# First batch of a spectral filter and a two-layer network: products kept whole, work shared out anew between Pool and DVE, one constant on another DMA queue

## The chip, the cores and the metric

One core of one Trainium2 chip. The time is the device time of one execution in microseconds (us), of which I give the median of a kernel's timed runs. The experiments ran in three groups of rounds, each on its own chip (e1 to e4, e5 to e8, e9 to e11), with the kernel before in every round, so times are compared within a group, and between groups only as ratios to the kernel before. Engines are named as in the profile: PE (matmul), DVE (VectorE), ACT (ScalarE), Pool (GpSimd), SP (which only issues DMAs here).

## The reference

A real FFT along the sequence, a product with a complex filter, the inverse FFT, then two dense layers with a leaky ReLU between them:

```python
# x: (8, 3008, 256), filt_r, filt_i: (1505, 256), w_in: (256, 2048), w_out: (2048, 256), all float32
X = np.fft.rfft(x, axis=1)
Y = X * (filt_r + 1j * filt_i)[None]
h = np.fft.irfft(Y, n=3008, axis=1).reshape(24064, 256) @ w_in
out = np.maximum(0.01 * h, h) @ w_out
```

## The kernel before

The transform of length 3008 is split as 94 x 32: matmuls with constant matrices (S1, S2, back with SA and SB), 32x32 transposes on DVE between them, the filter as an elementwise product between S2 and SA. Batches 1 to 7 go through these stages beside the dense layers of the batch before. Batch 0 has nothing to hide behind: its stages are the prologue, written by hand and in program order on every engine. Its 24 frequency groups come in two halves of the feature dimension (`hf` 0 and 1). For each half, PE makes S2 into PSUM; then the two products with `fa` and `fb` are taken either by DVE, straight from PSUM, or by Pool, after ACT has copied PSUM to SBUF; then PE makes SA from both products and ACT casts the result into `big[2]`; DVE transposes that (four transposes, two per half of the features), PE makes SB, and the dense layers begin.

PSUM has two wide buffers of two banks (`ph`) and three single banks (`pf`), used in turn; a matmul into one waits until the last reader of that buffer is done. Dummy matmuls (`keep_warm`) run while PE would stand still.

```python
    filt_load(fa_sb, filt_r, DH, DH, 64)               # the last of 12 filter pieces, all on Pool's queue
    filt_load(fb_sb, filt_i, DH, DH, 64)
    nc.gpsimd.dma_start(i1_sb[:], i1_d.ap())           # constant for SB, 752 KB
    nc.gpsimd.dma_start(w_in_sb[:], ...)
    # ... S1 of batch 0, with dummies ...
    t1_part(0, 0, True)(), t1_part(0, 1, True)()       # DVE: first transposes, half 0
    upper(0)                                           # fa copied on ACT, fb on DVE
    first_s2(0, 0, 8, False)                           # (half, first group, groups, on Pool?)
    first_s2(0, 8, 8, True)
    x_load(1)
    t1_part(0, 2, True)()
    keep_warm(4)
    first_s2(0, 16, 4, False)
    first_s2(0, 20, 4, True)
    t1_part(0, 3, True)()
    first_sa(0, 0), first_sa(0, 16)
    keep_warm(3)
    first_s2(1, 0, 8, False)
    first_s2(1, 8, 8, True)
    first_sa(0, 8), first_sa(0, 20)
    keep_warm(2)
    nc.gpsimd.dma_start(w_out_sb[:], ...)
    first_s2(1, 16, 8, False)
    first_sa(1, 0)
    keep_warm(4)
    first_t2(0), first_t2(1)                           # DVE: second transposes
    first_sa(1, 16), first_sa(1, 8)
    first_t2(2), first_t2(3)
```

## Time and profile before

| | before |
|---|---|
| median of 6 runs (us) | 782.97 (782.36 to 783.17) |
| span of the profiled run | 781.3 |
| first transpose of batch 0 starts at | 17.24 |
| last filter piece lands at | 28.21 |
| second transposes start at | 34.21 |
| first dense matmul at | 42.02 |

From 42 us on PE is the bound and hardly ever stops, so the table's last line is what a change of the prologue can move. The chain of waits and DVE's timeline are in the prediction.

### The profile page before, as it was taken

What the parts mean: (1) busy time and instruction counts of PE and PEld (TensorE: products, weight loads), DVE (VectorE), ACT (ScalarE), POOL (GpSimd) and SP (SyncE); (2) the same over time, 40 slices, a digit from 0 to 9 for tenths busy, and PEclk for the clock granted to TensorE, in tenths of its full rate; (3) what the DMA queues carried; (4) which work ended last, traced back from release to release, by engine and by line L of the source; (5) the groups of instructions that cost most, each with busy time, mean ns of one, the idle gap of its engine ahead of it and who ended that gap; (6) DMA issues with size and microseconds to landing.
All of it is one profiled execution on the core that took longest, in us unless ns stands there. A gap on an engine that the chain in (4) does not pass through costs nothing.

```text
span 781.3 us, 13416 instructions
## 1 busy us (share of the span) xinstructions
PE 772.2 (99%) x5716; PEld 524.0 (67%) x5716; DVE 367.4 (47%) x462; ACT 551.0 (71%) x784; POOL 152.2 (19%) x126
## 2 busy tenths in 40 slices
PE   9899999999999999999999999999999999999998
PEld 4366676666776677666777667766677666766666
DVE  4879751865238641577307754087432765200000
ACT  4587768676787767777587775967668776666664
POOL 5964300340004300042001410025000340000000
PEclk9999999999999999999999999999999999999999
DMA  9963002301041101510105010140101001100111
GB/s 183 228 107 78 32 28 64 86 30 40 33 102 42 42 28 42 108 42 28 41 28 122 28 40 30 41 107 28 42 29 41 28 28 42 41 35 34 41 41 55
DMA packets 39386, 44.15 MB, mean 57 GB/s; under 512 B 11266, under 2 KB 37506, under 8 KB 38658
## 3 DMA queue, kind: packets, MB, share of 16 engines
q0 software_dynamic: 13136, 17.78, 13.4%
q1 hardware_dynamic: 26192, 25.53, 9.3%
q8 instruction: 44, 0.72, 0.4%
q14 instruction: 14, 0.11, 0.1%
HBM read 35.67 MB, written 24.64 MB: 77 GB/s over the span
## 4 chain that ended last, share of the span: by engine, by line
PE 94%; DMA 2%; POOL 1%; ACT 1%; DVE 1%; issue 1%; POOLq 0%
PE ph L376 41%; PE po_ps L390 41%; PE pf L176 3%; PE pf L243 2%; PE pf L231 2%; PE pf L216 2%; DMA x_sb<-in_x_dram 1%; DMA fa_sb<-in_filt_r_dram 1%; PE pf L390 1%; POOL fy_h_c L276 1%; ACT big L187 0%; DVE big L297 0%; ACT big L290 0%; ACT gt_c L381 0%; PE ph L306 0%
## 5 line engine op out<-in xcount | busy, mean ns | idle before, releaser
L381 ACT ACTIVATE gt_c<-ph 128x1024 f16<-128x1024 f32 x376 | 384.8, 1023 | 195.6 <-PE ph L376 194.4
L376 PE MATMUL ph<-yt,w_in_sb 128*128 128x512 f16 (+3 forms) x1600 | 386.4, 366 | 0.3
L390 PE MATMUL po_ps<-w_out_sb,gt_c 128*128 128x256 f16 x2944 | 381.4, 272 | 0.5 <-ACT ost_c_t L397 0.5
L390 PEld LDWEIGHTS <-gt_c 128*128 128x128 f16 x3008 | 290.8, 98 | 89.2 <-issue 1.8
L376 PEld LDWEIGHTS <-w_in_sb 128*128 128x128 f16 x1600 | 154.5, 98 | 95.7 <-issue 0.4
L224 POOL TENSOR_TENSOR y_b_g<-p_b_g,p_b_g 128x512 f16<-128x512 f32 x84 | 106.8, 1271 | 225.4 <-DVE p_b_g L222 225.4
L199 DVE STREAM_TRANSPOSE big<-big 128x1024 f32<-128x1024 f32 x32 | 55.9, 1848 | 126.1 <-ACT big L187 126.1
L187 ACT CAST big<-pf 128x512 f16<-128x512 f32 x186 | 106.4, 604 | 1.8 <-PE pf L256 1.8
L246 DVE CAST yt<-pf 128x376 f16<-128x376 f32 x112 | 56.4, 545 | 86.0 <-PE pf L243 86.0
L220 DVE TENSOR_TENSOR p_b_g<-pf,fa_sb 128x512 f32<-128x512 f32 x84 | 58.1, 692 | 38.0 <-PE pf L216 35.4
L397 ACT COPY ost_c_t<-po_ps 128x256 f32<-128x256 f32 x184 | 69.3, 377 | 6.6 <-PE po_ps L390 5.4
L207 DVE STREAM_TRANSPOSE big<-big 128x1024 f32<-128x1024 f32 x28 | 51.1, 1939 | 34.1 <-ACT big L187 34.1
L221 DVE TENSOR_TENSOR p_b_g<-pf,fb_sb 64x512 f32<-64x512 f32 x84 | 58.2, 693 | 1.1
L222 DVE TENSOR_TENSOR p_b_g<-pf,fb_sb 64x512 f32<-64x512 f32 x84 | 57.4, 684 | 1.1
L132 POOL DMA_DIRECT2D x_sb<-in_x_dram x12 | 6.6, 553 | 253.1 <-PE pf L176 252.3
L243 PEld LDWEIGHTS <-big 128*128 128x128 f16 x448 | 25.6, 98 | 13.2
L176 PE MATMUL pf<-x_sb,f_sb 94*128 94x256 f16 x224 | 33.9, 272 | 0.2 <-DVE yt L246 0.2
L216 PE MATMUL pf<-big,small_sb 128*128 128x512 f16 x84 | 31.8, 379 | 0.0
L231 PE MATMUL pf<-y_b_g,small_sb 128*128 128x512 f16 x84 | 31.8, 379 | 0.0
L176 PEld LDWEIGHTS <-f_sb 94*128 94x128 f16 x224 | 21.5, 97 | 12.4 <-issue 0.4
L243 PE MATMUL pf<-i_sb,big 128*128 128x94 f16 x448 | 28.7, 206 | 0.0
L318 PE MATMUL po_ps<-idle 128*128 128x512 f16 x72 | 18.8, 405 | 1.2 <-DVE one L165 1.2
(46 smaller groups left out, 158.5 us busy)
## 6 DMA issues: line engine op xcount, KB each, us to landing
out_dram<-ost_c_t SPq DMA_DIRECT2D x92, 256.0 KB, 2.1
x_sb<-in_x_dram POOLq DMA_DIRECT2D x6, 1536.0 KB, 11.2
x_sb<-in_x_dram POOLq DMA_DIRECT2D x3, 480.0 KB, 9.8
fa_sb<-in_filt_r_dram POOLq DMA_DIRECT2D x6, 192.0 KB, 10.7
fb_sb<-in_filt_i_dram POOLq DMA_DIRECT2D x6, 192.0 KB, 8.6
w_in_sb<-in_moe_w_in_dram POOLq DMA_DIRECT2D x1, 1024.0 KB, 12.7
w_out_sb<-in_moe_w_out_dram POOLq DMA_DIRECT2D x1, 1024.0 KB, 12.7
x_sb<-in_x_dram POOLq DMA_DIRECT2D x1, 1024.0 KB, 8.1
```

What stands on the lines that cost most here:

```text
L176: nc.tensor.matmul(ps[:, j, :], f1_sb[:N1, n2, :], x_sb[:N1, n2, :], start=True, stop=True)
L187: copy(paired(dst)[:, ds(n0, nn), ds(e0, de)], ps.rearrange("p n (e t) -> p n e t", t=2))
L220: nc.vector.tensor_tensor(p1[:], ps, fa, AL.mult)
L221: nc.vector.tensor_tensor(p2[0:64], ps[64:P], fb[64:P], AL.mult)
L222: nc.vector.tensor_tensor(p2[64:P], ps[0:64], fb[0:64], AL.mult)
L224: nc.gpsimd.tensor_tensor(y1[:], p1[:], p2[:], AL.add)
L243: nc.tensor.matmul(ps[:, j, :], src[:, dt, n2, :], i1_sb[:, n2, :], start=True, stop=True)
L246: copy(yv[:, :, ds(4 * h, 4)], ps.rearrange("p c a -> p a c"))
L376: nc.tensor.matmul(ph[:, j, ds(o, ln)], w_in_sb[:, dt, ts(ct, P)], yt[:, dt, ds(lo, ln)], start=(dt == 0), stop=(dt == NDT - 1),)
L381: nc.scalar.activation(gts[ci][:, ds(2 * g, 2), :], ph, AF.Lrelu)
L390: nc.tensor.matmul(po, gts[ci][:, ct, ts(tj, P)], w_out_sb[:, ct, :], start=(ct == 0), stop=(ct == NCT - 1))
L397: nc.scalar.copy(ost[:, tj % 2, :], po)
```

## The change

The intent is to take load off Pool, which carried the middle of the prologue: Pool gets one chunk of eight groups per half and PE forms that chunk first; the rest of S2 goes to DVE in single banks; the products of a half stay together in the two buffers that the first dense layer uses later; the constant for SB leaves Pool's queue, and the issue of the weights comes after Pool's first products.

```diff
-    nc.gpsimd.dma_start(i1_sb[:], i1_d.ap())
-    nc.gpsimd.dma_start(w_in_sb[:], ...)
...
+    prods = [gtp.tile([P, 2, NC, DH], FP16, tag="gt", padded_shape=[P, 2, Q, DH], ...) for hf in range(2)]
...   # first_s2 takes the kind of PSUM buffer, writes prods[hf][:, i, ds(c, n), :]
     t1_part(0, 0, True)(), t1_part(0, 1, True)()
+    nc.vector.memset(i1_sb[:, 0, 0:2], 0.0)           # holds the load back until DVE is here
+    nc.sync.dma_start(i1_sb[:], i1_d.ap())
     upper(0)
+    first_s2(0, 8, 8, "ph", True)
+    nc.gpsimd.dma_start(w_in_sb[:], ...)
     t1_part(0, 2, True)()
+    first_s2(0, 0, 8, "ph")
+    for n0 in (0, N2 // 2):
+        x_load(1, n0, N2 // 2)
+    t1_part(0, 3, True)()
+    first_s2(0, 16, 4, "pf"), first_s2(0, 20, 4, "pf")
     keep_warm(4)
+    first_s2(1, 0, 8, "ph")
+    first_sa(0, 0, 8)
+    first_s2(1, 8, 8, "ph", True)
+    nc.gpsimd.dma_start(w_out_sb[:], ...)
+    first_sa(0, 16), first_sa(0, 20), first_sa(0, 8, 8)
+    first_s2(1, 16, 4, "pf"), first_s2(1, 20, 4, "ph")
+    first_sa(1, 0, 8)
     keep_warm(3)
     first_t2(0), first_t2(1)
+    first_sa(1, 16), first_sa(1, 20), first_sa(1, 8, 8)
     first_t2(2), first_t2(3)
...   # the old order removed
```

More of the change, by code (lines that the diff above doesn't have):

```diff
@@ L158 @@
     filt_load(fb_sb, filt_i, DH, DH, 64)
-    nc.gpsimd.dma_start(i1_sb[:], i1_d.ap())
-    nc.gpsimd.dma_start(w_in_sb[:], moe_w_in.rearrange("(dt p) c -> p dt c", p=P))
     idle = cpool.tile([P, CH], FP16, name="idle")
@@ L258, in first_s1, with first_s2 @@
         spread(big[0], n0, ps, copy)
-    def first_s2(hf, c, n, on_pool):
-        ps = bank("ph", n, DH)
+    prods = [gtp.tile([P, 2, NC, DH], FP16, tag="gt", padded_shape=[P, 2, Q, DH], name=f"prod{hf}")
+             for hf in range(2)]
+    def first_s2(hf, c, n, kind, on_pool=False):
+        ps = bank(kind, n, DH)
         src = paired(big[1])
@@ L267, in first_s2 @@
         fs = [f[:, ds(c, n), ts(hf, DH)] for f in (fa_sb, fb_sb)]
+        y = [prods[hf][:, i, ds(c, n), :] for i in range(2)]
         if on_pool:
-            y = [outp.tile([P, n, DH], FP16, tag="ost", name=f"fy{i}_h{hf}_c{c}") for i in range(2)]
             xs = [scrp.tile([P, 4, DH], FP32, tag=f"p{j // 4 + 1}", name=f"fx_h{hf}_c{c + j}")
@@ L277, in first_s2, with first_sa @@
         else:
-            y = [ypp.tile([P, n, DH], FP16, tag=f"yw{i}", bufs=2, name=f"fy{i}_h{hf}_c{c}")
-                 for i in range(2)]
             for i in range(2):
-                nc.vector.tensor_tensor(y[i][:], ps, fs[i], AL.mult)
-        ys[(hf, c)] = y
-    def first_sa(hf, c):
-        y = ys.pop((hf, c))
-        for j in range(0, y[0].shape[1], 4):
+                nc.vector.tensor_tensor(y[i], ps, fs[i], AL.mult)
+    def first_sa(hf, c, n=4):
+        y = [prods[hf][:, i, ds(c, n), :] for i in range(2)]
+        for j in range(0, n, 4):
             ps = bank("pf", 4, DH)
@@ L329 @@
     t1_part(0, 0, True)(), t1_part(0, 1, True)()
+    nc.vector.memset(i1_sb[:, 0, 0:2], 0.0)
+    nc.sync.dma_start(i1_sb[:], i1_d.ap())
     upper(0)
-    first_s2(0, 0, 8, False)
-    first_s2(0, 8, 8, True)
-    x_load(1)
+    first_s2(0, 8, 8, "ph", True)
+    nc.gpsimd.dma_start(w_in_sb[:], moe_w_in.rearrange("(dt p) c -> p dt c", p=P))
     t1_part(0, 2, True)()
-    keep_warm(4)
-    first_s2(0, 16, 4, False)
-    first_s2(0, 20, 4, True)
-    t1_part(0, 3, True)()
-    first_sa(0, 0), first_sa(0, 16)
-    keep_warm(3)
-    first_s2(1, 0, 8, False)
-    first_s2(1, 8, 8, True)
-    first_sa(0, 8), first_sa(0, 20)
-    keep_warm(2)
-    nc.gpsimd.dma_start(w_out_sb[:], moe_w_out.rearrange("(ct p) d -> p ct d", p=P))
-    first_s2(1, 16, 8, False)
-    first_sa(1, 0)
-    keep_warm(4)
+    first_s2(0, 0, 8, "ph")
[3 more added lines that the diff above has]
+    first_s2(0, 16, 4, "pf"), first_s2(0, 20, 4, "pf")
+    keep_warm(4)
+    first_s2(1, 0, 8, "ph")
+    first_sa(0, 0, 8)
+    first_s2(1, 8, 8, "ph", True)
+    nc.gpsimd.dma_start(w_out_sb[:], moe_w_out.rearrange("(ct p) d -> p ct d", p=P))
+    first_sa(0, 16), first_sa(0, 20), first_sa(0, 8, 8)
+    first_s2(1, 16, 4, "pf"), first_s2(1, 20, 4, "ph")
+    first_sa(1, 0, 8)
+    keep_warm(3)
     first_t2(0), first_t2(1)
-    first_sa(1, 16), first_sa(1, 8)
+    first_sa(1, 16), first_sa(1, 20), first_sa(1, 8, 8)
     first_t2(2), first_t2(3)
```

## The prediction

> **What bounds the kernel now.** I read the page first, for where the time is, then the chain of waits for the first 45 us, since every changed line lies there, then the timeline engine by engine from 19 to 42 us. The page:
>
> ```profile
> PE 772.2 (99%) x5716; PEld 524.0 (67%) x5716; DVE 367.4 (47%) x462; ACT 551.0 (71%) x784; POOL 152.2 (19%) x126
> PE 94%; DMA 2%; POOL 1%; ACT 1%; DVE 1%; issue 1%; POOLq 0%
> ```
>
> PE is busy 99% of the span and holds 94% of the chain that ended last; the rest of that chain, some 5%, is the prologue, in which the first batch goes through its transforms before the dense layers have anything to do. The first dense matmul starts at 42.02 us and from there PE rarely stops (before line 376 it waited 0.3 us in all). So whatever moves that start moves the end by as much, and nothing else in this change can. The chain of waits in the prologue (columns: start us, us, what):
>
> ```profile
> 12.00 9.73 DMA fa_sb<-in_filt_r_dram
> 22.02 0.70 POOL w_in_sb L160
> 22.83 3.07 POOL fy_h_c L276 x3
> 26.19 1.17 POOL fy_h_c L276
> 27.36 0.53 POOL x_sb L132
> 27.91 2.29 POOL fy_h_c L276 x2
> ...
> 33.08 1.23 DVE fy_h_c L281
> 34.76 2.13 ACT big L290 x4
> 36.92 2.38 DVE big L297 x2
> ```
>
> To be seen: Pool carries the middle. It can't issue the load of the weights before an older transfer (filter piece issued at 12.00) has landed at 21.73, its products start only at 22.83, and a chunk of four groups stands between the two chunks of eight. DVE, the other engine with products, meanwhile waits (timeline; in brackets, the idle time before and what ended it):
>
> ```profile
> 25.38 1.22 DVE L199 STREAM_TRANSPOSE big<-big 128x1024 f32<-128x1024 f32 x1
> 27.71 1.23 DVE L281 TENSOR_TENSOR fy_h_c<-ph,fa_sb 128x1024 f16<-128x1024 f32 x1 [1.11 <-PE ph L265]
> 31.94 1.22 DVE L281 TENSOR_TENSOR fy_h_c<-ph,fa_sb 128x1024 f16<-128x1024 f32 x1 [1.87 <-PE ph L265]
> 34.21 2.36 DVE L297 STREAM_TRANSPOSE big<-big 128x1024 f32<-128x1024 f32 x2
> 36.92 2.37 DVE L297 STREAM_TRANSPOSE big<-big 128x1024 f32<-128x1024 f32 x2 [0.34 <-ACT big L290]
> ```
>
> DVE lost 1.11 and 1.87 us waiting for a wide buffer to be filled; PE couldn't fill it because it stood, in its order, behind products of Pool. The last transposes (36.92) end the stage at 39.29; the third transform, 2.7 us of it, and the dense layer follow.
>
> **What the Trainium skill says.** "GPSIMD Engine Reference", Engine selection, puts a two-input elementwise operation on Pool at about half of VectorE's speed. This trace agrees: the 128x512 product takes 1.15 to 1.17 us on Pool, 0.65 to 0.67 on DVE. "DMA: Bandwidth & Descriptors", Issuing engines are not separate DMA queues, says that transfers from different engines run on the same 16 DMA engines and interleave. The trace before has no such overlap in the stretch that matters, but it shows the 16 engines full from 12 us on (about 180 GB/s, all of it filter pieces landing 1.1 us apart, the last at 28.21). "TensorE: Matmul & The Clock Gate", What's actually happening, says PE falls to half clock after an idle window of some 3.4 us. In this trace PE has no such gap and the granted clock is 1.00 in every 5 us stretch up to 50; I ask below whether the change opens one.
>
> **The change part by part.**
>
> (1) *Pool's load.* Twelve products become eight: 4 x 1.16 us = 2.3 us fewer; the issue of the inverse-transform constant (0.58) leaves Pool, and the issue of the weights (0.72) goes behind its first products. The chunk for Pool is now multiplied by PE first. Before, the first of two wide chunks was ready for DVE at 20.78, so Pool's copies by ACT can start there, not at 21.58; one copy takes 0.53, so Pool starts at 21.4 and has 4 products done at 21.4 + 4.6 = 26.0. Three issues (0.72 + 0.60 + 0.60) put it at 27.95.
>
> (2) *DVE's load.* It takes the 4 groups that Pool gave up and does its 8 last groups as two fours. In steps from start to start: eight groups 1.14, four groups 0.59, a transpose 1.17. From 19.64: a tiny memset and the copy of fb to 20.7; third transpose 21.85; two products of eight 24.15; fourth transpose 25.3; four products of four 27.7. That is the time at which DVE before restarted (27.71), now with the 4 extra groups done and nothing waited for. Two of eight: 30.0. Four of four: 32.3. So without a wait the next transpose could start at 32.3, against 34.21 before: 1.9 us. This is the intent of the change.
>
> (3) *ACT and the single banks.* All results and the small forward products now share three single banks, freed by ACT in order. I follow it with 0.55 us per ACT cast or copy, 0.43 per forward matmul, 0.21 per result matmul (two per group of four) and 0.2 of latency. PE can form the first wide chunk of half 1 after the fourth transpose: 25.4 to 26.3. Results of chunk 0: casts 26.95 to 28.05. Pool's second chunk is formed at 27.1 to 28.0; copies 28.25 to 29.3. Then casts of chunks 16 and 20: 29.9 and 30.45. The forward matmul for (half 1, chunk 16) reuses the bank of the cast that ends at 30.45, so DVE gets it at about 31.2, not at 30.0: **a new wait of 1.2 us on DVE**. Its four last products then run 31.2 to 33.5, and the transposes of half 0 start at 33.5: only 0.7 us earlier than before.
>
> (4) *Second half.* Pool starts at 28.85 and ends at 33.4 (before: 34.64). PE multiplies the last results at 34.0 to 34.85, ACT casts them until 35.8. DVE is then in its second transpose until 35.9, so the 0.34 us wait goes and the third and fourth run 35.9 to 38.3, against 36.92 to 39.29: 1.0 us earlier. The last stage starts its first half 0.7 earlier (after the second transpose) and its second half 1.0 earlier; ACT's casts follow the first, DVE's the second. I take the middle, 0.8 us.
>
> (5) *Transfers.* The constant (752 KB) goes by the SP queue at about 19.7 instead of behind the filters. Before it took 29.79 - 28.21 = 1.58 us; total bytes are the same, so if it interleaves, the last filter piece lands at 28.2 + 1.6 = 29.8 (estimate). DVE wants that piece at 28.85, so it waits 0.95 us and ends its two products at 30.95: still inside the wait of step 3, hence free. The weights, issued at 26.1, are still queued before the filters end and land at about 34.7 as before; needed at 41. The input of batch 1 follows, first half at about 38.4, second at 42; the first dense slots need only the first half. No loss, and no gain from the halves either.
>
> (6) *Buffers and dummies.* The products lie in the two buffers of the first layer's results, empty until 41 us and read for the last time at 34.85: free. Dummy matmuls fall from 72 to 69: off the path. Longest PE gap, after the four dummies until the fourth transpose: about 23.2 to 25.4, 2.2 us, under the skill's 3.4.
>
> Sum: -0.8 us on 782.53, so **781.7 us**.
>
> **Rivals.** (a) *DVE as the bound, no bank wait.* If ACT's casts run closer than I took them, DVE goes through and the full 1.9 us arrive: 780.6. For it: ACT is idle over half of the time from 20 to 35 us now. Against: its work is bunched at 27 to 31.5. (b) *The constant's transfer in front of the filters.* If the SP queue takes more than its share, or slows the 256-byte pieces beyond its own 1.58 us, every microsecond past a landing at 30.0 delays DVE by one. At 31.5, DVE ends its last products at 31.5 + 1.15 + 2.3 = 34.95, later than before by 0.7: 783.2. For it: the engines are full just there; against: the bytes are few. (c) *Hidden anyway.* The start could be held by a load: batch 1's input landed at 41.94 before, just ahead of its first use at 43.16. If its first half comes late, the gain is eaten: 782.5. Against: the first half needs half the bytes. (d) *A cold PE.* A gap over 3.4 us would double matmul times for a few microseconds: perhaps +1 us; the 2.2 us gap speaks against.
>
> **Range and chances.** (b) and (d) put the top at 783.1, (a) with some luck in the copies the bottom at 780.5. No rival comes near 2% (15.7 us), as the whole stage from 19 us to the dense layer is 22 us long and no transfer or operation grows by a multiple: faster 0.01, same 0.98, slower 0.01.
>
> **What the profile will show.** Right, if Pool's first product starts near 21.4 and its second chunk ends near 33.4; DVE has a wait of about 1 us on PE or a DMA before its last small products; the first pair of second transposes starts near 33.5, the other near 35.9; the first dense matmul starts near 41.2; and after it all stays in step. Wrong, if DVE waits for fb longer than 1 us (b), if its products run on without a wait (a), if the first dense matmul waits for a DMA (c), or if the granted clock leaves 1.00 (d). A difference from 42 us on would mean that I missed the mechanism altogether.

## More of the kernel before

One more view is needed later, the DMA queues between 24.0 and 25.5 us (columns: queue, packets, MB, time of the packets as a share of the 16 engines; it is over 100% here, so the times of packets overlap):

```profile
DMA packets 1077, 0.27 MB, mean 180 GB/s; under 512 B 1077, under 2 KB 1077, under 8 KB 1077
q0 software_dynamic: 1077, 0.27, 181.8%
```

Only Pool's queue (q0) is at work, and its data are the 256-byte rows of the filters.

## The result, and the profile after

| | before | after |
|---|---|---|
| median (us) | 782.97 | 783.01 (782.66 to 783.67, 6 runs) |
| ratio to before, 95% interval | | 1.0003 (0.9990 to 1.0016) |
| first transpose starts | 17.24 | 17.48 |
| last filter piece lands | 28.21 | 30.95 |
| second transposes start | 34.21 | 34.61 |
| first dense matmul | 42.02 | 42.40 |

A ratio here is the mean time of one kernel's runs over that of the other's in the same rounds, so not quite the ratio of the medians. The time did not move. In the fences of this and the next section, lines between those shown are left out. The first transposes depend on when batch 0's input lands, which differs between executions: in the thirteen profiles they start between 16.32 and 18.05 us. So below I judge by ratios and by waits in the trace, not by one absolute time.

Pool did what was planned (its timeline after):

```profile
21.62 2.27 POOL L278 TENSOR_TENSOR prod<-fx_h_c,fa_sb 128x512 f16<-128x512 f32 x2 [0.43 <-ACT fx_h_c L275]
29.03 2.28 POOL L278 TENSOR_TENSOR prod<-fx_h_c,fa_sb 128x512 f16<-128x512 f32 x2 [1.12 <-ACT fx_h_c L275]
31.27 2.26 POOL L278 TENSOR_TENSOR prod<-fx_h_c,fb_sb 128x512 f16<-128x512 f32 x2
```

It starts at 21.62 and ends at 33.5 instead of 34.64. It is no longer on the chain of waits of the prologue, which after the change reads:

```profile
5.59 13.82 DMA fb_sb<-in_filt_i_dram
19.69 11.26 DMA fb_sb<-in_filt_i_dram
31.07 1.24 DVE prod L281
33.41 1.28 DVE prod L281 x2
34.69 2.29 DVE big L296 x2
```

A filter piece now stands where Pool stood. DVE's timeline shows what it did:

```profile
27.22 0.67 DVE L281 TENSOR_TENSOR prod<-pf,fb_sb 128x512 f16<-128x512 f32 x1
28.90 1.23 DVE L281 TENSOR_TENSOR prod<-ph,fa_sb 128x1024 f16<-128x1024 f32 x1 [1.01 <-DMA fa_sb<-in_filt_r_dram]
31.07 1.22 DVE L281 TENSOR_TENSOR prod<-ph,fb_sb 128x1024 f16<-128x1024 f32 x1 [0.95 <-DMA fb_sb<-in_filt_i_dram]
32.22 0.68 DVE L281 TENSOR_TENSOR prod<-pf,fa_sb 128x512 f16<-128x512 f32 x1
34.61 4.86 DVE L296 STREAM_TRANSPOSE big<-big 128x1024 f32<-128x1024 f32 x4
```

DVE was at the end of half 0's products at 27.9, as planned, then waited 1.01 us for a piece of fa and 0.95 us for one of fb. The forward product for chunk 16 had been formed from 30.48 to 31.07, before DVE came to it at 32.22: the wait for a bank that I expected did not appear, it lay under the wait for the DMA. The same 1.5 us of the DMA queues as shown of before:

```profile
DMA packets 189, 0.59 MB, mean 393 GB/s; under 512 B 95, under 2 KB 95, under 8 KB 189
q1 hardware_dynamic: 94, 0.57, 94.7%
q0 software_dynamic: 95, 0.02, 15.7%
```

The two queues take turns packet by packet, 94 to 95. But a packet of the constant has 6016 bytes and takes 242 ns in the trace, one of the filters has 256 bytes and takes 40 ns (41 before). So the filters fall from 1077 packets to 95 while the constant passes. The Trainium skill ("DMA: Bandwidth & Descriptors", Queues, rings and completion order) says that each DMA engine round-robins between its queue rows at packet granularity; the counts of the trace, 94 to 95, agree. The page gives a packet 9 to 17 descriptors; whether what the trace counts as a packet is that, no run here shows.

The landings show the loss in one step. The pieces land about 1.1 us apart; among the last six, no step before was over 1.28. After, there is one from 23.59 to 26.66, that is 3.07 us, 2.0 longer than its neighbours. The constant's own engine time is 128 x 242 ns / 16 = 1.94 us. A smaller irregularity, a step of 2.47 followed by one of 0.63 (19.41, 21.88, 22.51), is not the constant's doing: a step of 2.16 and one of 2.07 stand at the same place in e1 and e7 below, where the constant is elsewhere. What makes it I can't say, but it counts: from the fourth piece to the sixth took 3.10 us here and 2.49 before, and in e5 and e11, which load the constant as the change does, 2.14 and 2.15. So this profile shows more lateness than the constant alone makes.

### The profile page after: what moved, and what is told of

Its sections match the earlier page's. It is cut to its first block, busy times and chain, and to the rows that moved or that the text cites. A ratio compares the mean times of both kernels' runs of the same rounds, so it can differ in the third digit from the quotient of the medians.

```text
span 781.9 us, 13405 instructions
## 1 busy us (share of the span) xinstructions
PE 770.7 (99%) x5710; PEld 523.5 (67%) x5710; DVE 368.6 (47%) x467; ACT 550.7 (70%) x783; POOL 150.2 (19%) x124
## 4 chain that ended last, share of the span: by engine, by line
PE 94%; DMA 3%; ACT 1%; DVE 1%; POOL 1%; issue 0%; DVEq 0%; POOLq 0%
PE ph L377 41%; PE po_ps L391 41%; DMA fb_sb<-in_filt_i_dram 3%; PE pf L174 3%; PE pf L241 2%; PE pf L229 2%; PE pf L214 2%; PE pf L391 1%; ACT big L185 0%; DVE prod L281 0%; DVE big L296 0%; POOL x_sb L132 0%; ACT yt L308 0%; PE ph L305 0%; ACT gt_c L382 0%
## 5 line engine op out<-in xcount | busy, mean ns | idle before, releaser
L317 PE MATMUL po_ps<-idle 128*128 128x512 f16 x66 | 17.0, 404 | 1.2 <-DVE one L163 1.2
```

## The experiments

Three theories were left. **A**: the constant on the SP queue takes the DMA engines from the last filter pieces, and DVE's wait for them eats the gain. **B**: the single banks, freed by ACT, hold DVE (step 3 of the prediction), and the landing is hidden behind that. **C**: PE's clock. The mean granted clock was under 1.000 in 5 of the 6 timed runs of the changed kernel, in 4 of them 0.998 or 0.997, though not in the one profiled. Some 3.4 us at half clock (as long as in e1 below) in a span of 781 would take 0.002 off the mean. The kernel before never had less than 0.999, in 27 runs of the rounds below. PE now has a gap of 2.07 us ahead of half 1.

**e1: the constant back behind the filters** (everything else of the change stays)

```diff
+    nc.gpsimd.dma_start(i1_sb[:], i1_d.ap())          # after the last filt_load
...
-    nc.vector.memset(i1_sb[:, 0, 0:2], 0.0)
-    nc.sync.dma_start(i1_sb[:], i1_d.ap())
```

> The changed kernel with one thing undone: the constant goes back to Pool's queue, behind the filter pieces (no memset, no SP load). Theory (the constant's 752 KB on the SP queue took the DMA engines from the last filter pieces, which landed at 30.95 instead of 28.21 us, and DVE waited 1.01 + 0.95 us for them): the last filter piece lands at 28.3 or so, DVE has no wait on a DMA, its wait on PE before the last small products comes back at about 1 us (it was hidden), second transposes start near 33.5 (changed kernel: 34.61), first dense matmul about 0.9 us earlier than in the changed kernel's 42.40; time about 782.1 to 782.3. Rival (the single banks, freed by ACT, are what holds DVE, the landing is hidden behind it): filters land early, DVE still starts its second transposes near 34.4, time unchanged at 783.0. Rival (start jitter only): everything within 0.3 us of the changed kernel.

Measured: 782.74 us against 783.37, ratio 0.9993 (0.9981 to 1.0006): in the direction of A, but less than expected, and not clear of noise. The last piece landed at 29.11; DVE's timeline:

```profile
29.23 1.23 DVE L282 TENSOR_TENSOR prod<-ph,fb_sb 128x1024 f16<-128x1024 f32 x1 [0.22 <-DMA fb_sb<-in_filt_i_dram]
31.77 0.69 DVE L282 TENSOR_TENSOR prod<-pf,fa_sb 128x512 f16<-128x512 f32 x1 [1.31 <-PE pf L268]
34.17 4.61 DVE L297 STREAM_TRANSPOSE big<-big 128x1024 f32<-128x1024 f32 x4
```

The DMA waits fell from 1.96 to 0.22 us, and the wait for a bank came out, 1.31 us. It is longer than forecast, and the stretches of this profile say why (columns: stretch and its length, busy us of PE, PEld, DVE, ACT, Pool, then the granted clock, DMA share and GB/s):

```profile
26.00:28.00 2.00, 2.00 (x7) 0.76 (x6) 2.00 (x5) 0.60 (x1) 1.85 (x4) 0.69 1.37 331
28.00:30.00 2.00, 2.00 (x7) 0.64 (x5) 1.78 (x2) 1.70 (x4) 0.44 (x1) 0.50 1.03 243
30.00:32.00 2.00, 2.00 (x9) 0.70 (x8) 0.69 (x2) 2.00 (x4) 2.00 (x3) 0.96 1.06 216
```

PE ran at half clock for 3.41 us (26.76 to 30.18 in the clock's own records), just where its matmuls feed ACT and DVE. So A and C are both there, and e1 mixes them.

**e2: the constant stays on SP, held back until DVE has taken its first products of half 1**

> The changed kernel, the constant still on the SP queue but gated by DVE one step later: its memset comes after the first products of half 1 instead of after the second transpose. Theory: filters land near 28.3, DVE's DMA waits are gone, constant is issued near 30 and lands near 33 to 35, before its use at 36; weights and batch 1's input land as in the changed kernel. Second transposes near 33.5, time 782.1 to 782.3 as in e1. Rival (it is the SP queue as such or the loss of Pool's pacing that slows the filters): filters land late here too, 783.0. Rival (constant becomes late for the last stage): PE waits for the constant at 36 us, time 783 or more.

Measured: 787.33 us, ratio 1.0055 (1.0042 to 1.0067). The filters landed early (27.56) and DVE had no DMA wait, as A says. But the constant, issued at 29.03, landed only at 39.85, and the profile's list of waits has:

```profile
PE pf L305 <- DMA i_sb<-inv_const: 5.0, 1, 5.0
```

That is the rival named for it; I had expected a landing at 33 to 35. Its first packet ran 3.6 us after the issue (in the changed kernel 3.9), and from then on it met batch 1's input on Pool's queue, whose packets took 624 ns against the constant's 242. Turn by turn, it no longer gets the engines almost alone. The queue is no fast lane: here it landed 10.8 us after its issue, in the changed kernel 6.6. PE, which stood 4.99 us for it, then also ran at half clock from 38.17 to 44.99, which is part of the 4 us lost.

**e3: e1 with the forward product of (half 1, chunk 16) ahead of the results of chunk 8**

```diff
-    first_sa(0, 16), first_sa(0, 20), first_sa(0, 8, 8)
-    first_s2(1, 16, 4, "pf"), first_s2(1, 20, 4, "ph")
+    first_sa(0, 16), first_sa(0, 20)
+    first_s2(1, 16, 4, "pf")
+    first_sa(0, 8, 8)
+    first_s2(1, 20, 4, "ph")
```

> e1, and the forward matmul of (half 1, chunk 16) goes ahead of the results of chunk 8 in PE's order, so that it takes a bank freed earlier. Theory of the prediction (bank wait of about 1 us once the DMA wait is gone): DVE's wait before its last small products falls to under 0.3 us for the first pair, second transposes start near 32.4 to 32.8, but the third transpose stays at ACT's casts of Pool's second chunk, near 35.4 to 35.9; first dense matmul 0 to 0.6 us earlier than in e1: time 781.7 to 782.2. Rival (ACT alone is the limit): second transposes start at the same time as in e1, no gain.

Measured: 782.28 us, ratio 0.9990 (0.9977 to 1.0002). The wait for that bank fell from 1.31 to 0.34 us, so B's mechanism exists; 0.61 us for the next product was new, since that one still stood behind the results of chunk 8. The second transposes started at 33.47, later than the 32.4 to 32.8 expected, the third at 36.40 behind ACT's casts. The clock was again at 0.50, from 26 to 28 us.

**e4: the constant on SP with no gate, at the very start**

> The changed kernel with the constant on the SP queue without any gate, so that it is loaded at the start, in front of batch 0's input. If the constant costs the DMA engines the time of its bytes wherever it stands in front of something awaited (128 packets of 242 ns over 16 engines: 1.94 us), batch 0's last input piece lands about 1.9 us later (15.3 to 17.2), the first transposes start at about 19.4, all later stages move by about 1.5 to 2 us less what the filters gain by standing behind it as before: time about 784 to 785. If instead input and constant share without loss (the input's packets being large too), the input lands under 1 us later: time 783.0 to 783.5.

Measured: 785.81 us, ratio 1.0037 (1.0021 to 1.0052). That is more than the 784 to 785 expected, and the place was not as expected either: batch 0's input landed at 15.97 (before: 14.84), not at 17.2. The constant itself landed at 17.47, and what moved most was the filter pieces behind it: the fourth landed at 21.47 instead of 19.24, and DVE and ACT waited 1.38 and 1.63 us for theirs. PE's gap grew to 3.40 us, and half clock from 27.53 to 30.94 followed; how much of the time is due to that was not tested.

**e5: the changed kernel with PE's gap filled**, thirteen dummies instead of four

```diff
     first_s2(0, 16, 4, "pf"), first_s2(0, 20, 4, "pf")
-    keep_warm(4)
+    keep_warm(13)
```

> The changed kernel with 13 instead of 4 dummy matmuls in PE's gap before the first forward product of half 1 (they fill some 1.9 us of a 2.07 us gap). Theory A (PE's clock falls to half for some 3.4 us around 25 to 30 us because of that gap; 5 of 6 timed runs of the changed kernel had a mean granted clock below 1.000, the run that was profiled didn't): clock 1.000 or 0.999 in all runs. Theory B (what holds the changed kernel is the late filter pieces, not the clock): the time stays within 0.4 us of the changed kernel, about 783.0, and DVE still waits about 2 us for DMA. If instead the clock is the cause of the lost gain, the time falls by 0.5 us or more.

Measured: 783.35 us against 783.32, ratio 0.9999 (0.9987 to 1.0012). The clock was 1.000 in all five runs, and the time that of the changed kernel. One filter step was again long, 2.96 us. But DVE waited for a DMA only once:

```profile
30.75 1.22 DVE L281 TENSOR_TENSOR prod<-ph,fb_sb 128x1024 f16<-128x1024 f32 x1 [0.91 <-DMA fb_sb<-in_filt_i_dram]
```

That is 0.91 us, not the 2 expected: this profile has no irregular step, and its transposes began 0.57 us later than in the first profile of the change. So the dummies cure the clock, and the clock is not what cost the gain here.

**e6: both, the constant behind the filters and the gap filled**

> e1 (constant behind the filters on Pool's queue) with the 13 dummies. Here the filters land early, so PE's half clock lies on the path: e1 had the granted clock at 0.50 from 27 to 30 us, DVE waited 1.31 us for the forward product of (half 1, chunk 16) and restarted 14.36 us after the first transpose. With the clock kept: clock 1.000, that wait falls to 0.8 to 1.0 us, second transposes 16.3 us after the first transpose instead of 16.76, first dense matmul about 0.3 to 0.5 us earlier than in e1, time 0.8 to 1.2 us under the kernel before. Rival (bank wait independent of the clock): same as e1, 0.6 us under the kernel before.

Measured: 782.31 us, ratio 0.9985 (0.9973 to 0.9998). On the same chip, in the same rounds, its slowest run (782.66) is below e5's fastest (783.05); the two differ in the constant's queue and its gate alone. DVE's timeline:

```profile
29.34 1.21 DVE L282 TENSOR_TENSOR prod<-ph,fb_sb 128x1024 f16<-128x1024 f32 x1
31.50 0.69 DVE L282 TENSOR_TENSOR prod<-pf,fa_sb 128x512 f16<-128x512 f32 x1 [0.96 <-PE pf L268]
```

No wait for DMA, and the bank's wait is 0.96 us instead of e1's 1.31. This is the state that the prediction described: 1.0 us gained, 0.8 forecast; in this profile 0.97 us of it lie between the first transposes and the first dense matmul (23.81 us, before: 24.78).

Not all of the difference to e5 lies in the prologue, though. The last matmuls of e5 and then of e6, under the span of each:

```profile
core 0 of [0], span 781.5 us
775.77 2.13 PE L391 MATMUL pf<-w_out_sb,gt_c 128*128 128x256 f16 x18
core 0 of [0], span 780.8 us
775.80 1.69 PE L390 MATMUL pf<-w_out_sb,gt_c 128*128 128x256 f16 x14
```

From the end of the last matmul to the end of the span e5 takes 3.63 us and e6 3.26. All seven profiles with the constant, or half of it, on SP have 3.62 or 3.63; the five with all of it behind the filters on Pool's queue have 3.25 or 3.26; the kernel before has 3.46. The last output landed equally soon after the last matmul in all (2.13 to 2.15 us), so the difference lies in what the program does to end; its cause was not sought. By the means of the timed runs e6 is 1.1 us under e5: 0.37 of that is this end, which leaves some 0.7 us for the late filters.

**e7: e6 with Pool's chunk formed first in half 1 too, and both small products ahead of the results of chunk 8**

```diff
+    first_s2(1, 8, 8, "ph", True)
+    nc.gpsimd.dma_start(w_out_sb[:], ...)
     first_s2(1, 0, 8, "ph")
     first_sa(0, 0, 8)
-    first_s2(1, 8, 8, "ph", True)
-    nc.gpsimd.dma_start(w_out_sb[:], ...)
-    first_sa(0, 16), first_sa(0, 20), first_sa(0, 8, 8)
+    first_sa(0, 16), first_sa(0, 20)
     first_s2(1, 16, 4, "pf"), first_s2(1, 20, 4, "ph")
+    first_sa(0, 8, 8)
```

> e6, and PE's order in half 1 changed: Pool's chunk is formed before DVE's (as the change does in half 0), and the two last small products are formed ahead of the results of chunk 8. By the theory of banks and order, DVE has no wait over 0.3 us from the second transpose of the input on: second transposes 15.2 to 15.6 us after the first transpose (before: 16.97, changed: 17.13), Pool's second chunk ends near 32.5, third transpose directly after the second; first dense matmul near 40 us; time about 2 us under the kernel before (ratio 0.9975). Rival (a load then holds the start: batch 1's input or the weights): first dense matmul or first use of the input waits for a DMA, gain 1 us or less.

Measured: 781.78 us against 783.32, ratio 0.9979 (0.9965 to 0.9993): the version that beats both.

```profile
28.11 1.21 DVE L282 TENSOR_TENSOR prod<-ph,fb_sb 128x1024 f16<-128x1024 f32 x1
29.25 0.67 DVE L282 TENSOR_TENSOR prod<-pf,fa_sb 128x512 f16<-128x512 f32 x1
31.64 2.35 DVE L297 STREAM_TRANSPOSE big<-big 128x1024 f32<-128x1024 f32 x2
34.85 2.37 DVE L297 STREAM_TRANSPOSE big<-big 128x1024 f32<-128x1024 f32 x2 [0.86 <-ACT big L290]
```

DVE runs through from its first transpose to its sixth without a wait; the second transposes start 14.97 us after the first (before: 16.97; 15.2 to 15.6 expected). But DVE then waits 0.86 us for ACT's casts ahead of the last two, where it waited 0.34 before, and that gives back 0.5 us of the 2.0. The ratio says 1.6 us, of which 0.2 are the shorter end. No load held the start.

**e8: the kernel before with the constant's move alone**

> The kernel before with one part of the change alone: the constant goes to the SP queue, gated as in the change. Theory: the filters land 2 to 2.7 us later here too (near 30.9), DVE waits for fb about 2 us in its first products of half 1, but it would have waited 1.87 us for PE (behind Pool) right after, so the end moves by only 0 to 0.4 us: time 783.0 to 783.7 when the kernel before is at 783.2. Rival (Pool's loss of the constant's issue brings a gain): Pool starts its products earlier, time 0.5 us or more under the kernel before.

Measured: 784.38 us against 783.32, ratio 1.0009 (0.9997 to 1.0022). The filters came late as expected (step of 3.05 us, last piece at 30.99), but I had expected the old wait for Pool to swallow the new one:

```profile
28.96 1.23 DVE L280 TENSOR_TENSOR fy_h_c<-ph,fa_sb 128x1024 f16<-128x1024 f32 x1 [1.67 <-DMA fa_sb<-in_filt_r_dram]
31.11 1.23 DVE L280 TENSOR_TENSOR fy_h_c<-ph,fb_sb 128x1024 f16<-128x1024 f32 x1 [0.93 <-DMA fb_sb<-in_filt_i_dram]
33.45 1.23 DVE L280 TENSOR_TENSOR fy_h_c<-ph,fa_sb 128x1024 f16<-128x1024 f32 x1 [1.11 <-PE ph L264]
```

PE can form the third chunk only when DVE has freed a wide buffer, so the wait is passed on. By this profile the second transposes start 17.79 us after the first instead of 16.97: the part alone costs 0.8 us, and another 0.16 at the end of the kernel. The timed ratio says 0.7 us, with an interval that just includes none.

**e9: half of the constant on SP, half behind the filters** (with e5's dummies)

> e5 (13 dummies), with half of the constant's rows on the SP queue, gated as in the change, and the other half on Pool's queue behind the filters as in e6. Size by dose: the full constant made one step between two filter landings 1.9 to 2.0 us longer (128 packets of 242 ns over 16 engines is 1.94); half of it should make that step 0.95 to 1.0 us longer, so that the last piece lands about 1 us later than in e6, near 29.5. DVE's wait for DMA falls to about 1 us or less and lies in front of the wait for a bank, which shrinks by as much: time as in e6, about 1.0 us under the kernel before, not half way. Rival (each microsecond of delay costs the same): half way between e5 and e6, about 0.5 us under the kernel before.

Measured: 782.49 us against 783.51, ratio 0.9990 (0.9977 to 1.0002). The long step is now 2.10 us, about 1.0 over its neighbours: half the bytes, half the delay. The last piece landed at 28.88. That is not the 29.5 expected (the run's filters began to land early, the fourth at 19.03), and DVE, ready at 28.94, lost nothing to it; its wait for the bank was 0.80 us. The time is that of e6 by medians (1.02 and 1.01 us under the kernel before). By ratios it lies between e6 (0.9985) and e5 (0.9999), about 0.4 us over the one and 0.7 under the other; 0.37 of the first is the longer end, which e9 shares with e5, so by this the prologue is about as fast as e6's. The intervals are too wide for the times alone to decide against half way, but the trace agrees: one microsecond of delay found room between the landing and DVE's need.

**e10: e7 without three dummies ahead of its last results**

> e7 without the three dummy matmuls ahead of its last results. In e7 the third transpose still waited 0.86 us for ACT's casts of those results, which PE formed after 0.65 us of dummies. If the dummies stand on that path, the wait falls to about 0.3 to 0.5 us and the time by 0.3 to 0.5 us against e7 (781.4 if e7 is 781.8). Rival (PE waits for the last products anyway, or its clock falls without the dummies): no gain, or a mean clock below 0.999.

Measured: 781.56 us against 783.51, ratio 0.9978 (0.9965 to 0.9992). The wait for ACT's casts fell from 0.86 to 0.39 us, but the ratio is that of e7 within a tenth of its interval. Whether the 0.3 to 0.5 us arrive is not resolved.

**e11: the changed kernel again, as a control**

> The changed kernel as it is, on the same chip and in the same rounds as the two others: a control. Ratio to the kernel before 0.999 to 1.001; mean granted clock below 1.000 in most runs; the last filter piece near 30.5 to 31, with one step between two landings near 3 us.

Measured: 783.35 us against 783.51, ratio 1.0003 (0.9990 to 1.0015), the same as the first time. One filter step of 3.16 us, last piece at 30.23. The mean clock was below 1.000 in two of five runs, not in most.

All of them, sorted by what they hold (times of the trace, in us, from each kernel's one profile; "end" is from the last matmul to the end of the span):

| run | constant | PE gap filled | longest step among the last six filter landings | second transposes after the first | end | ratio to before |
|---|---|---|---|---|---|---|
| before | behind filters | no such gap | 1.28 | 16.97 | 3.46 | 1 |
| after, e11 | SP | no | 3.07, 3.16 | 17.13, 16.03 | 3.62, 3.63 | 1.0003, 1.0003 |
| e5 | SP | yes | 2.96 | 16.23 | 3.63 | 0.9999 |
| e2 | SP, gated later | no | 1.12 | 16.87 | 3.63 | 1.0055 |
| e4 | SP, at the start | no | 1.16 | 18.21 | 3.63 | 1.0037 |
| e1 | behind | no | 1.25 | 16.76 | 3.25 | 0.9993 |
| e3 | behind, one product earlier | no | 1.19 | 16.27 | 3.25 | 0.9990 |
| e6 | behind | yes | 1.64 | 16.01 | 3.26 | 0.9985 |
| e9 | half and half | yes | 2.10 | 16.30 | 3.62 | 0.9990 |
| e7, e10 | behind, new order | yes | 1.30, 1.14 | 14.97, 14.97 | 3.25, 3.25 | 0.9979, 0.9978 |
| e8 | SP, order of before | no such gap | 3.05 | 17.79 | 3.62 | 1.0009 |

The fifth column shows a trap. DVE's sequence starts with its first transpose, but the filters land as the DMA queue gets to them. In e11 and e5 the transposes began late (18.02 and 18.05), so the filters were less late for them and less waiting shows (0.80 and 0.91 us); most of it replaces the wait for the bank. Where the last piece sets the pace, the start of the transposes no longer matters: the first dense matmul starts 11.45 us after that piece lands both in the first profile of the change and in e5 (11.63 in e11; e6 12.92, before 13.81). One profile of such a kernel can't size the loss; the timed rounds do.

## Why the prediction was right or wrong

**What bounds: right but for the end.** The dense layers are in step: from the start of their second group of matmuls to the last one 734.23 us before and 734.25 after. But "nothing else in this change can" move the end was not so: what follows the last matmul takes 3.62 us instead of 3.46, 0.16 us that the prediction did not have.

**Steps 1 and 2, Pool and DVE: right.** Pool's first product was forecast at 21.4 and came at 21.62, with all of the run 0.24 us later; its second chunk at 33.4 and 33.5. DVE reached the products of half 1 at 27.7 by forecast, at 27.9 in the trace.

**Step 3, ACT and the single banks: right in kind and nearly in size, but not visible in the changed kernel.** The wait of 1.2 us that I forecast shows as 0.96 in e6, where nothing else hides it, as 1.31 in e1 at half clock, and as none after the change, where a longer wait covers it. Order alone cuts it to 0.34 in e3 (where 0.61 for the next product is new) and removes it in e7.

**Step 4, the second half: right as it shows in e6**, where the third transposes follow the second without a wait.

**Step 5, transfers: this is the step that failed**, in the words "so it waits 0.95 us and ends its two products at 30.95: still inside the wait of step 3, hence free". Two terms were too small. The constant's delay was taken as 1.58 us, from how soon it landed after the last filter piece before. But there its first packets ran from 25.85 us on, while rows of the filters were moved until 27.64 (the prediction read that stretch as "all of it filter pieces"), so that difference hid part of its 1.94 us. And I let only the last piece wait: all pieces behind the constant were late, fa's last one too (28.77 instead of 25.84), so DVE waited twice, 1.01 + 0.95 us, and ended those products at 32.3. The wait of step 3 could have hidden it until 31.2, so DVE was 1.1 us late. Not all of that is the constant's: 0.24 us are the later start, and about 0.6 us more came from the irregular step (3.10 us instead of 2.49). In e5 and e11, which have no such step and whose transposes began later, the delay was mostly hidden. What the constant on SP costs on average is therefore read from the timed rounds: e6, which takes it off SP and changes nothing else of e5, is 1.1 us faster by the means, of which 0.37 us are the end and some 0.7 us the late filters. The ratios of e9 and e5, with the same end, give 0.7 us too. These 0.7 us, an estimate, and the 0.16 us of the end together make up for the 0.8 us forecast. Rival (b) of the prediction had the mechanism, at about the right landing, and I gave it too little weight.

**Rival (d), the cold clock**: set aside because of the 3.4 us of the skill, it did happen: in six of the eleven timed runs of the changed kernel the mean clock was 0.998 or less. It costs e1 about 0.35 us of DVE's wait (1.31 against 0.96), but in the changed kernel the late filters cover it, as e5 shows. Why a gap of 2 us does it at times can be read from the clock's records in the traces. From when it first became full (4.03 to 7.05 us) the clock changed only at multiples of 3.41 us: in e1 20.48 us full, 3.41 half, 750.93 full. Each half clock before the dense layers followed a period that held at least 2.05 us of the gap (2.12 in e1, 2.05 in e2, 2.11 in e3, 3.12 in e4). In the two profiles of the changed kernel a border of the periods cut the gap into 1.01 + 1.06 and 0.52 + 1.55 us, and the clock stayed full. So it would be luck whether a run is hit; that the timed runs differ for this reason is not shown, as they have no trace.

**Step 6, and the halves of batch 1's input**: no run waited for the product buffers, and none for that input. Whether the halves were needed was not tried. The dummies fall from 72 to 66, not to 69, which changes nothing.

**The number.** 781.7 us forecast, 783.01 measured, inside 780.5 to 783.1 but at its upper end: a change of nothing where a gain of 0.8 us was forecast. The forecast counted from 782.53, the median of the three runs of the kernel before that were known then; six give 782.97, so 0.4 us of the miss are the base. "Same" was right.

## What to carry to other kernels

A load moved to another DMA queue does not come for free beside one that is already full: here the queues took turns by packets, 94 to 95, so the load of large packets nearly stopped that of small ones for as long as its own bytes took. Put it behind what is awaited first, or count its full engine time against every piece behind it. And when a wait is forecast to hide another, compare their ends, not their lengths: half the constant, 1 us of delay, cost DVE nothing in e9's trace; the whole of it cost some 0.7 us in the timed rounds. Last, compare the two traces after the last common work too: moving one load to SP lengthened the end of the kernel here.

## What the Trainium skill lacked or had wrong

- "DMA: Bandwidth & Descriptors", Queues, rings and completion order, has the round-robin by packets, but not what follows for unequal packets: 94 of 6016 bytes (242 ns each) against 95 of at most 256 bytes (40 ns), and the filters' queue fell from 1077 packets to 95 in 1.5 us.
- "TensorE: Matmul & The Clock Gate", What's actually happening, has an idle window of about 3.4 us ahead of the half clock. Here gaps of 2.05 to 2.21 us were followed by 3.41 us of half clock in e1, e2 and e3: 2.05 us of idle time within one period of 3.41 us was enough, 1.55 us (e11) was not. Filled with nine more dummies, the mean clock was 1.000 in all five runs of e5.
- No page that I used says how much of a kernel's scatter comes from its first load. The first transposes started at 16.32 to 18.05 us in thirteen profiles, while batch 0's last input piece landed at 13.75 to 15.98.
- No page that I used says that a load on SP lengthens what follows the last matmul: 3.62 to 3.63 us in seven profiles with the constant on SP, 3.25 to 3.26 in five without.
